# A spectral filter and MLP kernel: the first batch's last on-chip turn stores neighbouring channels side by side, and the transform stage behind it uses full 128-column tiles

## The chip, the core and the metric

The kernel runs on one core of a Trainium2 chip. Its engines work side by side, each through its own queue of instructions: TensorE (matrix products; PE in the profile, with its weight loads as PEld), VectorE (DVE), ScalarE (ACT), GpSimd (POOL) and the queue that issues DMAs (SP). The metric is the device time of one launch in microseconds. Three runs of the kernel gave a median of 740.99 us, the lowest 740.27 and the highest 742.85.

## The reference

Input `x` has 8 batches of 3008 rows by 256 channels. Along the rows each batch goes through a real Fourier transform, a product with a complex filter, and the inverse transform; then each row goes through a two-layer MLP with 256, 2048 and 256 channels.

```python
X = np.fft.rfft(x, axis=1)
Y = X * (filt_r + 1j * filt_i)[None, :, :]
y = np.fft.irfft(Y, n=x.shape[1], axis=1)
h = y.reshape(24064, 256) @ w_in
out = np.maximum(0.01 * h, h) @ w_out
```

## The kernel before

**The transform.** 3008 is written as 94 times 32. A transform is two stages of small matrix products with a turn (a change of which index lies on the partitions) between them: `s1` (94 points), turn, `s2` (32 points), filter product, `sa` (inverse, 32 points), turn, `sb` (inverse, 94 points). The output of `sb` lands in `yt`, which holds channels on the partitions and rows along the free axis, as the MLP needs them.

**Two forms of it.** Batches 1 to 7 make their turns by DMA and run inside the MLP's work. Batch 0 has nothing to run beside: it is a prologue written out by hand as the list `FIRST` (lines 482 to 500), in which each entry is a step and its arguments, and every engine's queue has its instructions in the order of that list. Its turns are DVE transposes of 32x32 blocks: `t1` (line 396) between `s1` and `s2`, and `t2` (line 442) between `sa` and `sb`, four instructions each, of 128 partitions by 1024 fp32 words. A word is a pair of fp16 values, so that one transpose moves two values at a time.

**The steps that the change touches.** `sae` (line 438, engine ACT in all 12 entries of `FIRST`) copies a result of `sa` from PSUM to `big[2]` as fp16 pairs. `t2 i` turns a quarter of the channels from `big[2]` to `big[0]`: `t2 0` and `t2 1` make the first half of the channels (`dt` 0), `t2 2` and `t2 3` the second. `sb_matmuls` (line 447) reads `big[0]` as the stationary operand of the last stage, with the constant `i1_sb` streaming by (94 columns); it is called by `sbp` (line 456) in the prologue and by `late_sb` (line 464) afterwards. `sbe` and `quad_copy` (lines 461 and 345) copy a group from PSUM to `yt` on ACT or DVE. One group is four values of the index n2 for one half of the channels; batch 0 has 16, of which ten (eight with `dt` 0, two with `dt` 1) are in `FIRST` and six (`dt` 1) are put among the work of the MLP's first chunks by the list `REST` (lines 114 and 703).

**The order at the end of the prologue.** On DVE: the last filter products (`s2d`), `t2 1`, `t2 0`, `t2 3`, `t2 2`, then the copies `sbe 0 3` and `sbe 1 0`. On PE: the last `sa` products, four matmuls without use (`warm 4`, which only keep PE at work), the eight groups with `dt` 0, `sbp 1 0` and `sbp 1 1`, then the MLP. On ACT: the `sae` copies, then eight `sbe` copies with `sbe 1 1` last.

**After the prologue.** The MLP runs over 47 chunks of 512 rows (`moe1`, line 520, is its first layer). A planner gives each piece of work a time (8 units to a chunk) and issues the pieces in the order of these times, with `work` as a heap; the times set nothing but the order in each queue. The first matmul of `moe1` needs the groups 0 and 1 of `dt` 0 in `yt`, its second those of `dt` 1.

Of the kernel before, what the change touches and what calls it, by code (L numbers as in the profile page):

```python
# [13 lines left out]
FP32 = mybir.dt.float32  # L14
# [5 lines left out]
N1, N2 = 94, 32  # L20
NC = 24
Q = 32
# [56 lines left out]
def kernel(  # L79
# [9 lines left out]
    nc = tc.nc  # L89
# [46 lines left out]
    i1_sb = cpool.tile([P, N2, NW], FP16, name="i1_sb")  # L136
# [8 lines left out]
    big = [cpool.tile([P, Q * D + (HALF // 2 if i == 2 else 0)], FP16, name=f"big{i}") for i in range(3)]  # L145
# [144 lines left out]
    def paired(t):  # L290
        return t[:].rearrange("p (e n t) -> p n e t", n=Q, t=2)
# [5 lines left out]
    E4 = D // 2 // 4  # L297
# [77 lines left out]
    held, spare = {}, [scrp.tile([P, 4, DH], FP32, tag=f"p{i // 2 + 1}", name=f"spare{i}") for i in range(6)]  # L375
# [61 lines left out]

    def sae(hf, c, e):
        engine[e](paired(big[2])[:, ds(c, 4), ts(hf, DH // 2)],
                  held.pop(("sa", hf, c)).rearrange("p n (t e) -> p n e t", t=2))  # L440

    def t2(i):
        a = big[2][:].bitcast(FP32)[:, ts(i, E4 * Q)].rearrange("p (e n r) -> p e n r", n=Q // 2, r=2)
        o = big[0][:].bitcast(FP32).rearrange("p (h n e r) -> p h e n r", h=2, n=Q // 2, r=2)
        nc.vector.transpose(o[:, i // 2, ts(i % 2, E4)], a)

    def sb_matmuls(ps, dt, h):
        assert ("i1t",) not in issued
        src = big[0][:].rearrange("p (h n e r t) -> p h n r t e", h=2, n=Q // 2, r=2, t=2)
        for j in range(4):  # L450
            n2 = 4 * h + j
            for t in range(2):
                nc.tensor.matmul(ps[64 * t : 64 * t + 64, j, :], src[:, dt, n2 // 2, n2 % 2, t, :],
                                 i1_sb[:, n2, :N1], start=True, stop=True)

    def sbp(dt, h, b):
        ps = fill(("sb", dt, h), b, 4, NW)[:, :, :N1]
        held["sb", dt, h] = ps
        sb_matmuls(ps, dt, h)
# [4 lines left out]
    def late_sb(dt, h, copy):  # L464
        ps = bank("pf", 4, NW)[:, :, :N1]
        sb_matmuls(ps, dt, h)
        quad_copy(0, h, dt, ps, copy)
# [11 lines left out]
    def blank(i):  # L479
# [19 lines left out]
        sbe 0 3 D, sbe 1 0 D  # L499
    """  # L500
    steps = dict(s1p=s1p, s1e=s1e, t1=t1, s2p=s2p, s2d=s2d, s2a=s2a, s2m=s2m, sap=sap, sae=sae, t2=t2,
                 sbp=sbp, sbe=sbe, x=load_x, w_out=load_w_out, xc=round_x, warm=keep_warm, blank=blank)
    for step in FIRST.split(","):
# [227 lines left out]
    for b in range(1, B):  # L731
        z = 47 * (b - 4) if b > 4 else 0
        p = PLANS[min(b, 4) - 1]
# [23 lines left out]
    while queue:  # L757
        time, n, stage, b, g, f = heapq.heappop(queue)
        t = max(time, last + GAP)
# [64 lines left out]
```

## Time and profile before

| | |
|---|---|
| median of 3 runs | 740.99 us (740.27 to 742.85) |
| the profiled execution | 740.64 us |
| its span, first to last instruction | 738.8 us |
| PE busy | 730.5 us (99%) |
| ACT busy | 549.3 us (74%) |
| DVE busy | 508.7 us (69%) |
| granted TensorE clock, mean over the span | 1.000 |
| prologue, up to the first MLP matmul | 34.71 us |

The 1.8 us between span and time lie outside the instructions. A line of a group names the source line, the engine, the operation, what it writes and reads with the shapes, how often, then the busy time and the mean duration of one in ns, and the idle time ahead of it. The chain of waits follows the execution back from its last instruction; what lies on it sets the end.

### The profile page before, as it was taken

The numbers are of one execution on the slowest core, as the hardware profiler recorded it, in microseconds if no ns is written. First come the engines' busy times: TensorE is split into PE (matmuls) and PEld (weight loads), VectorE is DVE, ScalarE is ACT, GpSimd is POOL, SyncE is SP. The second block draws the span as 40 slices with busy tenths as digits, with TensorE's granted clock in tenths as the row PEclk, the third lists the DMA queues.
The fourth block names the chain that finished last, engine by engine and source line by source line (L and its number), as shares of the span: only waits on it lengthen the run. The fifth ranks groups of instructions, "written<-read, shape, count | busy, mean of one in ns | idle before, by whom it ended". The sixth has DMA issues, their size and how long they took to land.

```text
span 738.8 us, 19530 instructions
## 1 busy us (share of the span) xinstructions
PE 730.5 (99%) x8129; PEld 521.8 (71%) x8129; DVE 508.7 (69%) x696; ACT 549.3 (74%) x763; POOL 168.0 (23%) x171
## 2 busy tenths in 40 slices
PE   8999999999999999999999999999999999999997
PEld 3666677777777777777777777777767777777776
DVE  7878557776677667676777668666767676465566
ACT  4775787887788778887688777888767777777762
POOL 5605411333221312212132322222031220000000
PEclk9999999999999999999999999999999999999999
DMA  9978778778755595556855477434863433112012
GB/s 203 228 109 171 189 150 170 178 172 167 188 134 126 138 193 143 130 145 126 183 131 137 122 157 169 115 90 110 149 172 95 117 106 94 55 55 66 29 46 71
DMA packets 128617, 98.44 MB, mean 133 GB/s; under 512 B 59296, under 2 KB 107296, under 8 KB 128336
## 3 DMA queue, kind: packets, MB, share of 16 engines
q1 hardware_dynamic: 112905, 79.37, 42.0%
q0 software_dynamic: 15056, 17.50, 15.7%
q8 instruction: 63, 1.03, 0.6%
q10 hardware_dynamic: 567, 0.32, 0.2%
q14 instruction: 26, 0.21, 0.1%
HBM read 45.97 MB, written 35.65 MB: 110 GB/s over the span
## 4 chain that ended last, share of the span: by engine, by line
PE 93%; SPq 2%; DMA 2%; DVE 1%; ACT 1%; POOL 0%; issue 0%; POOLq 0%
PE ph L528 42%; PE pf L601 18%; PE po_ps L601 18%; PE pf L269 2%; PE pf L362 2%; PE pf L315 2%; PE pf L337 2%; PE pf L693 1%; DMA x_sb<-in_x_dram 1%; PE po_ps L693 1%; SPq L277 1%; SPq L587 1%; DMA p_b_g<-p_b_g 1%; PE po_ps L384 0%; PE pf L436 0%; ACT yt L351 0%
## 5 line engine op out<-in xcount | busy, mean ns | idle before, releaser
L531 ACT ACTIVATE gt_c<-ph 128x1024 f16<-128x1024 f32 x376 | 385.4, 1025 | 132.3 <-PE ph L528 125.5
L528 PE MATMUL ph<-yt,w_in_sb 128*128 128x512 f16 x1504 | 447.3, 379 | 0.2 <-ACT yt L351 0.2
L601 PEld LDWEIGHTS <-gt_c 128*128 128x128 f16 x2800 | 201.8, 98 | 97.9 <-issue 1.3
L330 POOL TENSOR_TENSOR y_b_g<-p_b_g,p_b_g 128x512 f16<-128x512 f32 x84 | 118.1, 1407 | 421.1 <-DMA p_b_g<-p_b_g 288.1
L601 PEld LDWEIGHTS <-big 128*128 128x128 f16 x2128 | 151.4, 98 | 65.9
L528 PEld LDWEIGHTS <-w_in_sb 128*128 128x128 f16 x1504 | 117.7, 98 | 4.4 <-DVE yt L351 0.4
L324 DVE TENSOR_TENSOR p_b_g<-pf,fb_sb 128x512 f32<-128x512 f32 x78 | 53.7, 688 | 33.8 <-PE pf L315 20.3
L601 PE MATMUL po_ps<-wt_sb,gt_c 128*128 128x128 f16 x704 | 71.8, 219 | 0.0
L601 PE MATMUL pf<-wt_sb,gt_c 128*128 128x128 f16 x688 | 69.3, 219 | 0.0
L601 PE MATMUL pf<-wt_sb,big 128*128 128x128 f16 x704 | 68.7, 219 | 0.0
L601 PE MATMUL pf<-w_out_sb,gt_c 128*128 128x128 f16 x720 | 68.1, 219 | 0.0
L351 ACT CAST yt<-pf 128x376 f16<-128x376 f32 (+9 forms) x136 | 58.1, 441 | 12.2 <-PE pf L362 8.5
L601 PE MATMUL po_ps<-w_out_sb,gt_c 128*128 128x128 f16 x688 | 65.7, 219 | 0.0
L601 PE MATMUL po_ps<-wt_sb,big 128*128 128x128 f16 x688 | 65.5, 219 | 0.0
L567 DVE TENSOR_TENSOR gt_c<-gt_c 128x2048 f16<-128x2048 f16 x43 | 56.9, 1322 | 1.0
L327 DVE TENSOR_TENSOR p_b_g<-pf,fa_sb 128x512 f32<-128x512 f32 x84 | 57.2, 681 | 0.2
L567 DVE TENSOR_TENSOR big<-gt_c,big 128x2048 f16<-128x2048 f16 (+1 forms) x45 | 56.4, 1254 | 0.0
L567 DVE TENSOR_TENSOR big<-big,gt_c 128x2048 f16<-128x2048 f16 (+1 forms) x45 | 56.3, 1252 | 0.1
L567 DVE TENSOR_TENSOR big<-gt_c 128x2048 f16<-128x2048 f16 (+1 forms) x46 | 56.3, 1224 | 0.0
L339 ACT CAST big<-pf 128x512 f16<-128x512 f32 x84 | 49.0, 584 | 9.3 <-PE pf L337 7.4
L270 ACT CAST big<-pf 128x384 f16<-128x384 f32 x90 | 43.0, 479 | 11.5 <-PE pf L269 8.2
L362 PE MATMUL pf<-i_sb,big 128*128 128x94 f16 x448 | 37.0, 206 | 0.0
(98 smaller groups left out, 644.7 us busy)
## 6 DMA issues: line engine op xcount, KB each, us to landing
p_b_g<-p_b_g SPq DMA_DIRECT2D x156, 128.0 KB
out_dram<-ost_c_h SPq DMA_DIRECT2D x118, 128.0 KB
dz<-big SPq DMA_DIRECT2D x42, 256.0 KB
big<-dz SPq DMA_DIRECT2D x56, 192.0 KB
x_sb<-in_x_dram POOLq DMA_DIRECT2D x40, 192.0 KB, 4.2
x_sb<-in_x_dram POOLq DMA_DIRECT2D x2, 768.0 KB, 9.2
w_in_sb<-in_moe_w_in_dram POOLq DMA_DIRECT2D x1, 1024.0 KB, 13.1
w_out_sb<-in_moe_w_out_dram POOLq DMA_DIRECT2D x1, 1024.0 KB, 14.3
```

Source lines behind the costliest of these rows:

```text
L269: nc.tensor.matmul(ps[:, j, :], x_sb[:, 4 * h + j, ts(dt, P)], fwd1m[:, :NW], start=True, stop=True)
L270: copy(turn_in[:, :, dt, :, ds(4 * h, 4)], ps.rearrange("p n (q k) -> p k q n", q=4))
L324: nc.vector.tensor_tensor(p2[:], ps, fb, AL.mult)
L327: nc.vector.tensor_tensor(p1[:], ps, fa, AL.mult)
L330: ("y", b, g), lambda: nc.gpsimd.tensor_tensor(y1[:], p1[:], p3[:], AL.add)))
L339: nc.scalar.copy(st2[h % 3][:, ds(2 * (g % 2), 2), :], ps)
L351: copy(yt[:, dt, ds(to, 4 * n)].rearrange("p (a c) -> p a c", c=4), v[:, ds(a, n)])
L362: nc.tensor.matmul(ps[:, j, :], z2[h % 3][:, j, ts(dt, P)], i1_sb[:, 4 * h + j, :N1], start=True, stop=True)
L528: nc.tensor.matmul(ph[:, j, :], w_in_sb[:, dt, ts(ct, P)], yt[:, dt, ds(ci * CH % RING, CH)], start=(dt == 0), stop=(dt == NDT - 1))
L531: nc.scalar.activation(gts[ci][:, ds(2 * g, 2), :], ph, AF.Lrelu)
L567: nc.vector.tensor_tensor(*(v[:, ds(c0, n)] for v in (o, i0, i1)), op)
L601: nc.tensor.matmul(of[t], a()[:, c, ts(t, P)], w[:, c, :], start=(c == 0), stop=(c == NCH - 1))
```

## The change

Three places of the prologue's second half are rewritten. `sae` pairs the channels 2e and 2e+1 of its half of the channels, where it paired e and e+64; what it writes is the same set of addresses, what it reads from PSUM comes in order. `t2` writes its words in the order half, n2, e; before, two neighbouring values of n2 (r) lay side by side, in the order half, n2/2, e, r. So before, a DVE transpose stored 8 bytes (two words) at one place and then went 512 bytes on; now it stores 4 bytes (one word) and goes 256 bytes on. In `big[0]` the 128 channels of a half are now next to each other for each n2, so that `sb_matmuls` takes them as one stationary operand of 128x128 with the output on all 128 partitions of PSUM, where it took two of 128x64 (every fourth value), one for each 64 partitions. A group is four matmuls with four weight loads, where it was eight with eight. The number and order of the steps in `FIRST` and `REST` stay.

```diff
     def sae(hf, c, e):
         engine[e](paired(big[2])[:, ds(c, 4), ts(hf, DH // 2)],
-                  held.pop(("sa", hf, c)).rearrange("p n (t e) -> p n e t", t=2))
+                  held.pop(("sa", hf, c)).rearrange("p n (e t) -> p n e t", t=2))
 
     def t2(i):
-        a = big[2][:].bitcast(FP32)[:, ts(i, E4 * Q)].rearrange("p (e n r) -> p e n r", n=Q // 2, r=2)
-        o = big[0][:].bitcast(FP32).rearrange("p (h n e r) -> p h e n r", h=2, n=Q // 2, r=2)
+        a = big[2][:].bitcast(FP32)[:, ts(i, E4 * Q)].rearrange("p (e n) -> p e n", n=Q)
+        o = big[0][:].bitcast(FP32).rearrange("p (h n e) -> p h e n", h=2, n=Q)
         nc.vector.transpose(o[:, i // 2, ts(i % 2, E4)], a)
 
     def sb_matmuls(ps, dt, h):
         assert ("i1t",) not in issued
-        src = big[0][:].rearrange("p (h n e r t) -> p h n r t e", h=2, n=Q // 2, r=2, t=2)
+        src = big[0][:].rearrange("p (h n d) -> p h n d", h=2, n=Q)
         for j in range(4):
-            n2 = 4 * h + j
-            for t in range(2):
-                nc.tensor.matmul(ps[64 * t : 64 * t + 64, j, :], src[:, dt, n2 // 2, n2 % 2, t, :],
-                                 i1_sb[:, n2, :N1], start=True, stop=True)
+            nc.tensor.matmul(ps[:, j, :], src[:, dt, 4 * h + j], i1_sb[:, 4 * h + j, :N1], start=True, stop=True)
```

## The prediction

> **What bounds the kernel now.** I read the page first: which engine is full, and who carries the chain that ended last.
>
> ```profile
> PE 730.5 (99%) x8129; PEld 521.8 (71%) x8129; DVE 508.7 (69%) x696; ACT 549.3 (74%) x763; POOL 168.0 (23%) x171
> ...
> PE 93%; SPq 2%; DMA 2%; DVE 1%; ACT 1%; POOL 0%; issue 0%; POOLq 0%
> ```
>
> PE has 8.3 us without work in 738.8. Whatever lengthens or shortens PE's queue, or delays its start, therefore comes through to the end. The change touches only the prologue and six groups after it, so the next view is the chain of waits around the prologue's end (start, length, what):
>
> ```profile
> 27.90 1.22 DVE prod L416
> 29.11 2.29 DVE big L445 x2
> 31.45 0.46 PE pf L453 x8
> 31.93 2.74 ACT yt L351 x7
> 34.71 0.38 PE ph L528
> 35.09 0.38 PE ph L528
> ```
>
> The chain is not on PE here. It goes through two of the four transposes of `t2` (L445), one group of the last stage (L453), seven copies on ACT (L351), and then the MLP starts. The other two transposes run beside the ACT copies; the timeline of DVE shows how close behind they are:
>
> ```profile
> 30.19 3.55 DVE L445 STREAM_TRANSPOSE big<-big 128x1024 f32<-128x1024 f32 x3
> 33.66 0.51 DVE L351 CAST yt<-pf 128x376 f16<-128x376 f32 x1
> 34.35 0.55 DVE L351 CAST yt<-ph 128x376 f16<-128x376 f32 x1 [0.17 <-ACT yt L351]
> ```
>
> The fourth transpose ends at 33.74 (30.19 + 3.55), 1.35 us before the MLP's second matmul (35.09), which needs the last DVE copy. So all four transposes are within about a microsecond of the chain.
>
> **The transposes.** This term decides the sign. Their price, from the groups of the first 60 us:
>
> ```profile
> L416 DVE TENSOR_TENSOR prod<-ph,fa_sb 128x1024 f16<-128x1024 f32 x6 | 7.1, 1220 | 0.8 <-PE ph L408 0.6
> L445 DVE STREAM_TRANSPOSE big<-big 128x1024 f32<-128x1024 f32 x4 | 4.7, 1222 | 0.0
> L295 DVE CAST big<-pf 128x512 f16<-128x512 f32 x4 | 2.7, 688 | 0.5 <-PE pf L390 0.5
> L416 DVE TENSOR_TENSOR prod<-pf,fa_sb 128x512 f16<-128x512 f32 x4 | 2.5, 673 | 0.0
> L295 DVE CAST big<-ph 128x1024 f16<-128x1024 f32 x2 | 2.5, 1225 | 0.6 <-PE ph L390 0.6
> L351 DVE CAST yt<-pf 128x376 f16<-128x376 f32 x2 | 1.1, 531 | 0.0
> ```
>
> L416 with 512 and 1024 elements gives (1220 - 673) / 512 = 1.07 ns an element and 0.13 us fixed. L445 lies on the same line: 1024 words in 1222 ns. It stores two words at a place, so it opens a new place in SBUF every 2.14 ns. L295 also stores 4 bytes (two fp16 values) and then jumps, a place every 2.1 ns at full pace. None of the DVE rows that I read here opens places in SBUF faster than that. After the change each word is a place of its own.
>
> Lower end: the pace stays, nothing is added. L351 speaks for it: it reads PSUM with a jump at every element and still takes 376 x 1.07 + 0.13 = 0.53 us. A gain is left out, since L445 already runs at the pace of the in-order rows with fp32 on one side. Upper end: places open no faster than every 2.14 ns; 1024 of them take 2.19 + 0.13 = 2.32 us, 1.09 us more for each, 4.37 us for four. I take the upper end: L445 itself and L295 are stores into SBUF, as the changed instruction is, while L351's jumps are reads from PSUM. For two of the four I would have cover if only the first pair were on the chain; but DVE runs all four one after the other, and with 1.09 us more for each the fourth ends at 33.74 + 4.37 = 38.11. The groups with `dt` 0 and their seven ACT copies (2.74 us in the chain) begin 2.18 later than now, the copies at 34.1, so they are done by 36.9 and lie beside the second pair. The whole 4.37 is on the path.
>
> The Trainium skill bears on this term (Advanced Engine Details and Errata, section Memory Cachelines): SBUF has lines of 16 bytes, at least two accesses to a line are needed to hide its latency, and a new line for every access costs extra. It speaks against the change, with no figure; by it the four transposes cost something above nothing, and by the row alone the sum could also be the lower end's. No run shown so far has such a store.
>
> **Behind the fourth transpose.** Queued behind it on DVE are `sbe 0 3` and `sbe 1 0`; PE waits for it with `sbp 1 0` and `sbp 1 1`; SP and POOL have nothing waiting there. The stretch from its end to the MLP's second matmul stays, less what the shorter group saves, 0.10 us (from one execution of eight at 0.43 us to four at the 0.33 us of L269's form).
>
> **The late groups.** A piece of PE's queue with one group, before, and the same stage of a later batch, which already has four matmuls of 128x128:
>
> ```profile
> L453 PEld LDWEIGHTS <-big x128: 134/156/161, 31.4 to 80.1; 128*64 128x64 f16 x128
> ...
> 71.92 0.37 PE pf L453 x8
> ```
>
> ```profile
> L362 PEld LDWEIGHTS <-big x448: 97/98/99, 107.3 to 705.1; 128*128 128x128 f16 x150
> ...
> 107.54 0.17 PE pf L362 x4
> ```
>
> So each late group gives PE 0.37 - 0.17 = 0.20 us back. Six of them: 1.2 us. Two (at 41.4 and 45.8) stand ahead of or inside a stretch where the chain leaves PE for ACT and DVE (42.59 to 46.35), and I count them at nothing; that leaves 4 x 0.20 = 0.80. If the short wait for ACT at 69.3 also eats the two ahead of it, 0.40 is left. The other eight groups in the prologue lie beside the second pair of transposes: nothing.
>
> **The copies `sae`.** They read PSUM in order where they read with a jump. L295 on ACT has that read and the same store, 0.66 to 0.67 us for 128x512 against L439's 0.62 to 0.64. Bounds: 12 x 0.04 = 0.5 us more ACT work or none. It lies beside DVE's filter products and the first pair of transposes (ACT's last one ends at 31.34, the third transpose would start at 33.6). Without that cover it would be 0.04 us for the last copy. I count nothing.
>
> **Sum.** 4.37 - 0.10 - 0.80 = +3.47 us on the profiled execution's 740.64 (span 738.8, and 1.8 around it): 744.1 us. That execution is 0.35 below the median of 740.99, so the median may come out at 744.4. About 0.3%, 2.2 us, is what a measurement of this kernel can tell from no change.
>
> **Rivals.**
>
> *The transposes keep their pace.* A store that jumps at each word costs what L351's reads do. Then the chain goes as now, 0.10 us shorter at the first group, and the late groups give 0.80: 739.7 us, not slower. It decides from an added 0.9 / 4 = 0.23 us a transpose downwards. Against it: no row of SBUF stores with single words. Chance 0.18.
>
> *Part of the price.* Opening a place costs more, but half as much as the bound (0.55 us each, 2.2 in all), or part of the delay is absorbed behind the prologue: 2.2 - 0.9 = +1.3, 741.9 us. Against the absorbing: ACT's and DVE's queues start the MLP's work from the same point as PE, so the stretch from 42.59 to 46.35 moves with them, and the x loads and weights land early enough now. Chance 0.10.
>
> *The clock falls while PE waits.* With slow transposes PE has nothing from 31.24 (end of the four warming matmuls) to about 33.6, then 3 us of sparse groups, then about a microsecond of nothing. At the start of the trace, after idling, PE's weight loads of the warming matmuls come every 0.43 us (at 1.60, 2.02, 2.45 and so on to 5.44) and afterwards seven in 1.41 us: half rate for about 4.2 us. If that happened again at the MLP's start, 4.2 us would do 2.1 us of work: 744.1 + 2.1 = 746.2 us. Against it: no gap of the prologue now is over 0.4 us once PE has begun, so the trace does not show what one of 2.4 us does. Chance 0.10. The Trainium skill (TensorE: Matmul & The Clock Gate, Part 1) has the rate drop after a whole idle window of about 3.4 us; this gap would be shorter, which speaks against this rival.
>
> **How the numbers follow.** The forecast has 0.62; its own range is 743.0 to 745.0, from what the late groups give (0 to 1.2) and 0.1 us a transpose either way. The range for the time leaves out the rival in which the transposes keep their pace and the lower part of the partial price: 741.2 to 746.3 holds 0.62 + 0.10 + 0.08 = 0.80. Slower by over 0.3% (above 743.2 on the profiled time): 0.55 of the forecast, all of the clock's 0.10, 0.01 of the partial price: 0.66. Faster by over 0.3% needs more than the rival's 0.9 us: 0.03. Within 0.3%: 0.31.
>
> **What would show it.** L445 at about 2.3 us each, the fourth ending near 38.1, the MLP's second matmul at about 39.4 where it was 35.09; L453 with 64 instructions of 128x128 and weight loads of 98 ns; late groups of 0.17 us on the chain. The forecast is wrong if L445 stays at 1.2 us, if the MLP's second matmul moves by clearly less than the transposes grew, or if matmuls behind the gap are spaced at half rate.

## The result, and the profile after

Over 22 runs each the changed kernel has a median of 743.09 us and the kernel before 740.74: the ratio is 1.0032, with a 95% interval of 1.0025 to 1.0039, or about 2.35 us slower. The time lies inside the predicted range and on the predicted side; the forecast was 744.1 for the profiled execution, 1.2 us too high, and 744.4 for the median, 1.3 too high. Whether the loss is over the 0.3% bound the interval leaves open. The ratios in this document go by fast executions alone: one execution of a kernel below, `warm_gap2`, took 1544.55 us and is left out of its ratio.

The profiled execution took 742.86 us (span 741.0, so 2.2 more than before). First the two lines of the page that were shown of before: engines, and the chain by engine.

```profile
PE 729.8 (98%) x8065; PEld 521.1 (70%) x8065; DVE 513.3 (69%) x696; ACT 549.5 (74%) x763; POOL 167.0 (23%) x171
...
PE 91%; DMA 4%; DVE 2%; ACT 1%; POOL 1%; SPq 1%; issue 0%; POOLq 0%; DVEq 0%
```

PE has 64 matmuls fewer, and the chain gives DVE 2% where it gave 1%. Then the chain around the prologue's end (start, length, what; the last stage is now line 451, the MLP's matmul line 525, its activation line 528):

```profile
29.09 7.16 DVE big L445 x4
...
36.30 0.34 PE ph L451 x4
...
36.84 0.48 ACT yt L351
...
37.36 0.38 PE ph L525
...
38.43 0.32 PE pf L269 x4
38.75 0.85 PE ph L525 x2
```

All four transposes are on the chain, as forecast. They take 7.16 us where they took 4.63 (29.11 to 33.74): 2.5 us more, not 4.37. One of them takes 1.90 us in the median, before 1.22 (shortest, median and longest in ns):

```profile
L445 DVE STREAM_TRANSPOSE big<-big x4: 1874/1900/1972, 29.0 to 34.4; 128x1024 f32<-128x1024 f32 x4
```

The MLP's second matmul starts at 37.36, before at 35.09. Behind it is something that the sum did not have: from about 38 two matmuls of 512 columns take 0.85 us and four of 96 columns 0.32, where before they took 0.43 and 0.17. That is half rate. The windows show it as the granted clock. A row has the window and its length, then the busy time and the number of instructions of PE, PEld, DVE, ACT and POOL, and behind these five the clock:

```profile
34.00:38.00 4.00, 2.01 (x24) 1.22 (x24) 3.17 (x4) 2.35 (x6) 0.00 (x0) 1.00 1.11 190
38.00:42.00 4.00, 4.00 (x25) 2.20 (x24) 2.63 (x4) 2.21 (x3) 1.03 (x2) 0.57 1.44 200
```

and the second window in the kernel before:

```profile
38.00:42.00 4.00, 4.00 (x42) 2.25 (x40) 3.42 (x6) 4.00 (x7) 0.54 (x1) 1.00 1.42 202
```

The clock is 0.57 between 38 and 42 us, with 25 matmuls where before there were 42. PE was busy for only 2.01 of the 4 us ahead of it.

The late groups are the third part. One of them, on the chain of the changed kernel:

```profile
74.82 0.17 PE pf L451 x4
74.99 0.22 PE po_ps L690 x2
```

and the answering piece of the kernel before:

```profile
71.92 0.37 PE pf L453 x8
72.29 0.32 PE po_ps L693 x2
```

The group takes 0.20 us less, as forecast, and the piece behind it 0.10 less, which was not: after two tiles of 128x64 the next two matmuls took 0.32 us, after full tiles 0.22.

How these parts add up can be read from the starts of the MLP's activations, the same work in all kernels. A plus is the delay against the kernel before. The first activation stands at 36.16 before and at 38.53 after (+2.37), the fifth at 40.91 and 44.76 (+3.85), the 41st at 111.69 and 114.08 (+2.39). So the transposes, with the stretch behind them, cost 2.3 to 2.4 (2.27 at the MLP's second matmul), the half rate a further 1.5, and the late groups give 1.5 back. Later single waits for DMAs and for POOL move the two executions against each other by 0.2 to 1.3 us. They come at other places in other executions: in the kernel before, PE waits 1.2 us for POOL near 540 us, which the changed kernel does not.

### The profile page after: what moved, and what is told of

It is laid out like the page before. It is cut to its first block, busy times and chain, and to the rows that moved or that the text cites. A ratio compares the mean times of both kernels' runs of the same rounds, so it can differ in the third digit from the quotient of the medians.

```text
span 741.0 us, 19402 instructions
## 1 busy us (share of the span) xinstructions
PE 729.8 (98%) x8065; PEld 521.1 (70%) x8065; DVE 513.3 (69%) x696; ACT 549.5 (74%) x763; POOL 167.0 (23%) x171
## 4 chain that ended last, share of the span: by engine, by line
PE 91%; DMA 4%; DVE 2%; ACT 1%; POOL 1%; SPq 1%; issue 0%; POOLq 0%; DVEq 0%
PE ph L525 42%; PE pf L598 18%; PE po_ps L598 18%; PE pf L362 3%; PE pf L337 2%; PE pf L315 2%; PE pf L269 2%; DMA fa_sb<-in_filt_r_dram 1%; PE pf L690 1%; PE po_ps L690 1%; DMA fa_sb<-in_filt_i_dram 1%; DVE big L445 1%; ACT gt_c L528 1%; DVE prod L416 1%; DMA big<-dz 1%; SPq L277 1%
## 5 line engine op out<-in xcount | busy, mean ns | idle before, releaser
L528 ACT ACTIVATE gt_c<-ph 128x1024 f16<-128x1024 f32 x376 | 385.1, 1024 | 133.9 <-PE ph L525 127.0
L598 PE MATMUL pf<-wt_sb,gt_c 128*128 128x128 f16 x688 | 69.3, 219 | 0.0
L564 DVE TENSOR_TENSOR big<-gt_c 128x2048 f16<-128x2048 f16 (+1 forms) x46 | 58.3, 1268 | 0.0
```

The costliest lines, as they stand in the source:

```text
L528: nc.scalar.activation(gts[ci][:, ds(2 * g, 2), :], ph, AF.Lrelu)
L564: nc.vector.tensor_tensor(*(v[:, ds(c0, n)] for v in (o, i0, i1)), op)
L598: nc.tensor.matmul(of[t], a()[:, c, ts(t, P)], w[:, c, :], start=(c == 0), stop=(c == NCH - 1))
```

## The experiments

**The price of the store alone.** The kernel before with 16 more transposes in a stretch of DVE's queue.

```diff
+    def probe(i):
+        w = big[0][:].bitcast(FP32)
+        a = big[1][:].bitcast(FP32)[:, : E4 * Q]
+        # o: one of eight patterns of the same 1024 words in w
...
+        nc.vector.transpose(o, a)
-        s2p 0 12 4 1 b4, t1 2, s2d 0 8 4 1,
+        s2p 0 12 4 1 b4, t1 2, probe 0, probe 1, ..., probe 7, probe 7, ..., probe 0, s2d 0 8 4 1,
```

> The kernel before, with 16 more transposes on DVE ahead of the first s2d, each of 128x1024 words from big[1] into big[0], which t2 overwrites later; eight ways to store, each twice, in the order 0 to 7 and back. 0: two words at a place, places 512 bytes apart (before). 1: one word, 256 bytes apart (after). 2: one word, 512 bytes apart. 3: two words in one 16-byte line, 8 bytes apart from each other. 4: two neighbouring words, but every second pair across the border of two 16-byte lines. 5: words in order. 6: one word, 16 bytes apart. 7: four neighbouring words at a place. Theory 'line' (a store that opens a new 16-byte line with each word costs extra, two words in a line are enough): 0, 3, 5, 7 at 1.2 us, 1, 2, 6 at 1.9, 4 between them at about 1.55. Rival 'neighbours' (8 bytes must lie together): 3 at 1.9 and 4 at 1.2, the others as above. Rival 'distance' (banks or the stride decide): 1 and 2 differ, and 6 is near 1.2.

Timeline of its DVE queue, patterns 0 to 4 and 6 in order (start, length); 5 and 7 took 1.25 us:

```profile
19.11 1.25 DVE L509 STREAM_TRANSPOSE big<-big 128x1024 f32<-128x1024 f32 x1
20.39 1.95 DVE L509 STREAM_TRANSPOSE big<-big 128x1024 f32<-128x1024 f32 x1
22.38 1.92 DVE L509 STREAM_TRANSPOSE big<-big 128x1024 f32<-128x1024 f32 x1
24.33 1.25 DVE L509 STREAM_TRANSPOSE big<-big 128x1024 f32<-128x1024 f32 x1
25.61 1.49 DVE L509 STREAM_TRANSPOSE big<-big 128x1024 f32<-128x1024 f32 x1
...
28.41 1.98 DVE L509 STREAM_TRANSPOSE big<-big 128x1024 f32<-128x1024 f32 x1
```

The second pass, in reverse order, repeats this within 0.05 us. Theory "line" holds at every point: one word at a place costs 1.90 to 1.98 us at distances of 256, 512 and 16 bytes; two words in one line of 16 bytes cost 1.25 whether they touch or not; pairs of which every second one crosses the border of a line cost 1.49. "Neighbours" would have made the fourth pattern slow, and "distance" pattern 6 fast. The Trainium skill (Advanced Engine Details and Errata, section Memory Cachelines) says as much: lines of 16 bytes, and two accesses to a line needed. The price here is 0.65 to 0.73 us for 1024 words. With the added work the one execution of this kernel took 766.82 us.

**PE kept at work in the gaps.** The changed kernel with more warming matmuls.

```diff
-        ... sae 1 0 A, warm 4, sbp 0 1 b1,
+        ... sae 1 0 A, warm 10, sbp 0 1 b1,
-        ... sbp 0 5 b3, sbp 1 0 b4,
+        ... sbp 0 5 b3, warm 5, sbp 1 0 b4,
```

> The changed kernel with ten warming matmuls instead of four ahead of the first group of the last stage, and five more ahead of sbp 1 0; both fall into PE's idle time. Theory 'the clock fell in the gap and cost 1.5 us': the MLP's first matmuls come every 0.22 us from the start, the first MLP activation stands at about 38.5 as in the changed kernel but the third is 1.5 us earlier, and the time is 1.5 us below the changed kernel's 743.1, at about 741.6, a ratio of 1.0012. Rival 'the half rate was that one execution's or has another cause': no gain, 1.0032.

Measured: 740.6 us, ratio 1.0007 (0.9998 to 1.0015). The window that had 0.57:

```profile
38.00:42.00 4.00, 4.00 (x39) 2.34 (x38) 3.67 (x6) 3.40 (x5) 1.32 (x2) 1.00 1.41 200
```

Full clock and 39 matmuls. The transposes are as slow as in the changed kernel (7.29 us for four), the first activation is at +2.32, the fifth still at +2.32, the 41st at +0.86. So the half rate, and not something else behind the transposes, is the 1.5 us. Its share shows in the times as well: 1.0032 against 1.0007, with intervals that do not touch.

**Which gap.** The same two fillings apart (`warm 10` alone, and `warm 5` ahead of `sbp 1 0` alone).

> The changed kernel with ten warming matmuls instead of four ahead of the first group of the last stage; the second idle stretch of 1.5 us ahead of sbp 1 0 stays. If the second stretch is what lets the clock fall, the half rate stays (first MLP matmuls 0.43 us apart, ratio 1.0032); if PE's work over both stretches together decides, the clock stays up and the ratio is that of both fillings, 1.0007.

> The changed kernel with five warming matmuls ahead of sbp 1 0 alone; the first idle stretch of 1.0 us ahead of the first group stays. If the second stretch is the cause: full rate, ratio 1.0007. If the first one starts it: half rate, 1.0032.

With the first filling alone the ratio is 1.0016 (1.0003 to 1.0030), with the second alone 1.0005 (0.9991 to 1.0019). The window of 38 to 42 us, first of the first, then of the second:

```profile
38.00:42.00 4.00, 4.00 (x27) 2.24 (x26) 2.16 (x4) 1.51 (x2) 0.58 (x2) 0.61 1.44 196
```

```profile
38.00:42.00 4.00, 3.65 (x38) 2.06 (x35) 3.08 (x6) 2.50 (x4) 1.09 (x2) 1.00 1.48 199
```

In these two traces the second gap is the one that matters: PE's idle time of about 1.5 us ahead of `sbp 1 0`, which the slow second pair of transposes makes. The first, of 1.0 us in the changed kernel and 1.64 in the second of these two, does not bring the half rate by itself. The two intervals overlap, so the ratios alone do not decide it.

Two measurements say more. The first is the mean granted clock of every execution. In the 81 executions of the kernel before that ran beside these kernels it is never under 0.999; the changed kernel's profiled execution, with its one stretch of half rate, has 0.998. Taken as the sign of half rate, a clock of 0.998 or less is found in 21 of the changed kernel's 22 executions, in none of the 12 of `after_warm`, in 6 of 10 with the first filling alone, and in 1 of 9 with the second alone. Those 6 took 742.5 to 743.9 us, the other 4 took 740.1 to 741.2. So the same kernel gets the half rate in some executions and not in others, and both fillings make it rarer. (Nine of the changed kernel's executions have 0.995 or 0.996, more than one such stretch explains; no trace of one was kept.)

The second is when the clock changes. In the changed kernel it rises at 3.98 us, falls at 38.12 and rises at 41.53: the last two are 3.41 us apart, the first two ten times that. In every trace here the changes lie on such steps of 3.41 us, counted from the first rise, which comes at 3.98 to 7.16 us and so differs between executions. The step ahead of the fall and the step of half rate, in the changed kernel:

```profile
34.70:38.12 3.42, 1.53 (x18) 0.89 (x17) 2.58 (x4) 1.65 (x5) 0.00 (x0) 1.00 1.15 187
38.12:41.53 3.41, 3.41 (x20) 1.87 (x18) 2.51 (x4) 1.74 (x2) 0.66 (x2) 0.50 1.46 199
```

After the first rise, each step of the twelve traces in which PE was busy for 1.62 us or less is followed by half rate, and none with 1.67 us or more is (1.51 in the first of these two kernels; 1.77 in the second, with its gap of 1.64 us). So in these traces PE's work within one step decides, and not one gap by itself; a gap counts by where it lies in the steps.

**A gap in the kernel before.** Its four warming matmuls are left out.

```diff
-        ... sae 1 0 A, warm 4, sbp 0 1 b1,
+        ... sae 1 0 A, sbp 0 1 b1,
```

> The kernel before without its four warming matmuls, which makes an idle stretch of some 1.3 us on PE ahead of the first group. Theory 'a stretch of one to one and a half us without PE work is enough for the half rate': MLP's first matmuls at 0.43 us for some 3 us, about 1.5 us more, ratio 1.0020. Rival 'it takes longer or sparser work than that': no half rate, ratio 1.0000.

Measured: ratio 1.0011 (1.0000 to 1.0022), and 1.00 as the granted clock from 38 to 42 us; the first, the fifth and the 41st activation stand at +0.73, +0.73 and +0.71. So no half rate in the profiled execution, and no execution of the ten has a mean clock under 0.999. This execution was late for another reason: POOL's last product and ACT's copies stood ahead of the third transpose on the chain. PE's idle pieces there were 0.49 and 0.56 us, shorter than I had expected, so that this kernel did not make the gap it was meant to make. Whether its 0.8 us are the missing matmuls' doing stays open.

**The new store with the old tiles.**

```diff
-                  held.pop(("sa", hf, c)).rearrange("p n (e t) -> p n e t", t=2))
+                  held.pop(("sa", hf, c)).rearrange("p n (t e) -> p n e t", t=2))
...
-        src = big[0][:].rearrange("p (h n d) -> p h n d", h=2, n=Q)
+        src = big[0][:].rearrange("p (h n e t) -> p h n t e", h=2, n=Q, t=2)
         for j in range(4):
-            nc.tensor.matmul(ps[:, j, :], src[:, dt, 4 * h + j], i1_sb[:, 4 * h + j, :N1], start=True, stop=True)
+            n2 = 4 * h + j
+            for t in range(2):
+                nc.tensor.matmul(ps[64 * t : 64 * t + 64, j, :], src[:, dt, n2, t, :],
+                                 i1_sb[:, n2, :N1], start=True, stop=True)
```

> The changed kernel's stores in t2 (one word at a place), but channels e and e+64 paired as before and the last stage in two tiles of 128x64 as before. Theory 'the transposes cost 2.4 us, the full tiles give back some 1.6 us in the late groups': late groups at 0.37 us and 0.1 us more for the piece of PE's queue behind them, as before; 1.6 us above the changed kernel if the clock falls here too, 744.7 or a ratio of 1.0054, and about 743.2 or 1.0033 if PE's longer groups keep the clock up. Rival 'the full tiles give only the 0.20 us of their own row': 0.8 us above the changed kernel with the same clock, 1.0043.

Measured: 743.69 us, ratio 1.0048 (1.0029 to 1.0067), too wide to choose between the cases by the time alone. The half rate is there (0.59 from 38 to 42 us). The first activation stands at +3.43, the fifth at +4.35. The first is higher than the changed kernel's because the transposes start 0.27 us later in this execution (29.36) and because the half rate begins at 37.83, so that a part of its cost lies ahead of the first activation. The 41st stands at +3.91. A late group of its chain, and the weight loads:

```profile
76.00 0.29 PE pf L453 x8
76.29 0.33 PE po_ps L693 x2
```

```profile
L453 PEld LDWEIGHTS <-big x128: 106/113/123, 33.1 to 84.0; 128*64 128x64 f16 x128
```

Here I had a detail wrong: I expected 0.37 us for a late group, and it is 0.29. With the new store the 64 channels of a tile lie every 4 bytes, before every 8, and a weight load of them takes 113 ns, not 156. So the late groups' 1.46 us (the fifth to the 41st activation) come in two parts: 0.44 from the closer channels, which this kernel already has, and the other 1.0 from the full tiles, about half of that in the piece behind the group, which keeps its 0.33. The Trainium skill (TensorEngine Tiling (Array Packing), section Key Properties) says that changing the tiling mode drains TensorE; the 0.10 us behind each group agree with that, but no run here shows that the drain is their cause.

**Half the change.** The channels with `dt` 1, whose last stage is mostly in the late groups, get the new store and full tiles; those with `dt` 0 stay as before.

```diff
     def t2(i):
+        if i < 2:     # dt 0: pairs of words, tiles of 128x64
+            a = a.rearrange("p (e n r) -> p e n r", n=Q // 2, r=2)
+            o = o.rearrange("p (n e r) -> p e n r", n=Q // 2, r=2)
+        else:         # dt 1: single words, tiles of 128x128
+            a = a.rearrange("p (e n) -> p e n", n=Q)
+            o = o.rearrange("p (n e) -> p e n", n=Q)
```

> Half the change: the channels with dt 1 (second pair of transposes, two groups in the prologue and the six late ones) as in the changed kernel, those with dt 0 as before. Theory: the second pair takes 1.2 us longer, its end comes at about 35.0 and the MLP's second matmul at about 36.2 (35.09 before); the late groups give 1.6 back and the clock stays up since the gap is short: 740.3, a ratio of 0.9995. Rival 'the clock falls also in a gap of half the length': up to 1.5 more, 1.0015.

> Half the change (dt 1 alone with single-word stores and full tiles), once more beside the next kernel: 0.9992 of the kernel before, 739.5 to 740.3.

Measured twice: 739.53 us with a ratio of 0.9992 (0.9983 to 1.0002), and 740.26 with 0.9992 (0.9982 to 1.0003). The transposes in the chain of the first:

```profile
29.04 6.06 DVE big L452 x4
```

Their end at 35.10 and the clock at 1.00 are as expected, but the reason that was given for the clock, a short gap, is wrong. PE's gap ahead of `sbp 1 0` is as long as in the changed kernel:

```profile
35.15 0.34 PE L460 MATMUL ph<-i_sb,big 128*128 128x94 f16 x4 [1.57 <-DVE big L452]
```

What differs is the work around it: in the two 3.41 us steps over the gap PE was busy for 2.31 and 2.39 us. In other executions the clock did fall. The mean clock is 0.998 or less in 5 of the 23 executions of both runs. The median of these 5 is 741.46 us, that of the other 18 is 739.43. So the rival is right for some executions.

The first and the fifth activation stand at +1.13, the 41st at -0.35. The delay is half of the changed kernel's, the gift of the late groups is whole. Beyond the 41st nothing of it should change, and 0.35 us of 740 (0.05%) is too little for these two runs to tell from nothing.

**PE's gap filled with work.** On top of the half, the `dt` 0 matmuls of the MLP's first four column tiles are issued in PE's gap.

```diff
+    def ahead(ct):
+        nc.tensor.matmul(wide[ct // 2][:, ts(ct % 2, CH)], w_in_sb[:, 0, ts(ct, P)], yt[:, 0, :CH],
+                         start=True, stop=False)
...
-        for dt in range(NDT):
+        for dt in range(1 if ci == 0 and ct < 4 else 0, NDT):
```

> Half the change as in the kernel hybrid, and PE's idle time ahead of sbp 1 0 filled with useful work: the first-half (dt 0) matmuls of the MLP's first four column tiles are issued there, and moe1 leaves them out; for that sbe 0 3 goes to ACT, and three groups take other PSUM banks. Theory: the second pair of transposes still ends at about 35.1, four matmuls of 0.215 us are off PE's queue behind it: 0.86 us below hybrid's 739.5 to 739.8, at about 738.8, a ratio of 0.9980. Rival 'ACT and DVE set the pace in the stretch behind the prologue and eat it': no gain over hybrid, 0.9992.

> Half the change, and the dt 0 matmuls of the MLP's first four column tiles issued in PE's idle time ahead of sbp 1 0 (moe1 leaves them out); in difference to hybrid_ahead sbe 0 3 stays on DVE, so that ACT has no ninth copy, and the group 0 5 goes to the bank of 0 7, 1 0 to that of 0 6, 1 1 to that of 0 5. Theory: the MLP's second-half matmuls begin at about 36.2 as in hybrid, and four matmuls of 0.215 us less stand behind them: 0.86 us below hybrid, a ratio of 0.998. Rival 'ACT and DVE set the pace in the stretch behind the prologue': first MLP activations 0.4 us earlier, but by the stretch around 44 us the lead over hybrid is gone, 0.9992.

In `hybrid_ahead` the copy of group 0 6 reads its PSUM bank after group 1 1 has overwritten it, so it computes wrong values there; the amount of work is the same. It took 740.26 us (0.9993; 0.9984 to 1.0002): moving `sbe 0 3` to ACT put a ninth copy on ACT, and PE waits for it. The timeline of its PE:

```profile
37.26 0.38 PE L544 MATMUL ph<-yt,w_in_sb 128*128 128x512 f16 x1 [1.31 <-ACT yt L351]
```

`hybrid_fill` leaves that copy on DVE: 740.04 us, ratio 0.9988 (0.9979 to 0.9996), the one kernel here whose interval lies wholly below 1. But it does not show the 0.86 us: its fifth activation is at +1.11, hybrid's at +1.13. Its chain says why:

```profile
37.40 0.89 ACT gt_c L547
...
38.31 1.02 ACT gt_c L547
39.33 0.37 ACT big L270
39.70 1.02 ACT gt_c L547
```

From 37.4 on ACT is the chain, one activation after the other, as the rival said. The other half of the rival, first activations 0.4 us earlier, did not come: the first stands at +1.24, hybrid's at +1.13. In this execution the third transpose waited for ACT copies that stood behind a late product of POOL, and the four end at 35.42, hybrid's at 35.10. Counted from the MLP's second-half matmuls (36.54 here, 36.21 in hybrid) the fifth activation comes after 5.47 us, in hybrid after 5.82: of the 0.86 us, 0.35 are kept up to there. Whether they last to the end stays open: against hybrid the difference of the ratios (0.0004) is within both intervals, and a part of it may be the clock, which is not under 0.999 in any execution of `hybrid_fill`.

## Why the prediction was right, and where it was not

The sign and the place are right: the new store makes the transposes slower, the four stand one behind the other on the path that starts the MLP, and all of their delay comes through. That the sum came near is partly luck: two errors cancel in part. The transposes' term was 1.9 us too large, and a half rate of 1.5 us that the sum did not have stood in its place. With the measured price alone the sum would have been 2.5 - 0.10 - 0.80 = +1.6 us. Of the signs of being wrong that the prediction names, one came: matmuls behind the gap at half rate. The wide range had room for such a mixture; the forecast's own range did not hold the profiled 742.86 us. That range was also mis-added: its two terms (0.4 us either way for the transposes, 0 to 1.2 for the late groups) give 743.3 to 745.3, not 743.0 to 745.0. And 743.2 is 0.3% above the median; above the profiled time it is 742.9.

*The transposes (4.37 forecast, 2.5 measured).* The step that failed is the upper end: "places open no faster than every 2.14 ns". That was the pace at which two words at a place happen to be stored, 2 x 1.07 ns, and not a limit on opening places. At one word a place the 1024 words take about 1.9 us, so a place opens every 1.73 ns ((1.90 - 0.13) / 1024). The rows bounded the price on both sides correctly, and the value lay between: the rival "part of the price" with 0.55 us each was nearer than the forecast (about 0.63 each here).

*Behind the fourth transpose (0.10 forecast, 0.24 measured).* From the end of the transposes to the MLP's second matmul it took 1.11 us (36.25 to 37.36), before 1.35. The mechanism held, and the size was off: before, the MLP's first matmul itself stood behind the ACT copies (34.71) and the second 0.38 behind it; now those copies are long done, the first matmul runs ahead, and only the last copies count.

*The clock (0 forecast, 1.5 measured).* I had this as a rival against the forecast, at 0.10 and with 2.1 us. It happened in the changed kernel's profile, together with the middle price of the transposes, and by the mean clock in 21 of its 22 executions; `after_warm` shows that work in the gaps removes it. The working had weighed the length of one gap of 2.4 us; with the faster transposes that gap was 1.0 us, and the second, of 1.54 us, which the working had put at "about a microsecond", left PE 1.53 us of work in the 3.41 us step ahead of the fall. The sentence on the Trainium skill (TensorE: Matmul & The Clock Gate, Part 1) pointed the wrong way here: by a whole idle window of about 3.4 us no drop was to come, and the measurement decides.

*The late groups (0.80 forecast, 1.46 measured).* The 0.20 us of the group's own row were right. Missing was the 0.10 in the next piece of PE's queue, and I counted four groups where five came through (between the fifth and the 41st activation the delay falls five times, by 0.29 to 0.32 us each, and rises once by 0.10): only the one inside the ACT- and DVE-bound stretch gave nothing, and the two ahead of 69.3 us gave theirs in full.

*`sae`.* Counted at nothing, and nothing it is: L439 takes 620 ns after, 618 before.

Put together, +2.37 at the first activation, +1.48 and -1.46, which is +2.39 at the 41st and close to the 2.35 of the medians.

## What to carry to other kernels

Look at what one instruction stores into each 16-byte line of SBUF: a DVE transpose of fp32 words that leaves a single word in each line runs some 50 to 60% longer, and two words in the line, touching or not, are enough to keep the pace. When a change delays a stage, ask what the engine that waits does meanwhile: a matmul engine with a gap ahead of its long stretch may start it at half rate, and here a few matmuls in the gap, useful or not, prevented it. Judge this by the clock of several executions: the same kernel had the half rate in some and not in others. When only part of the data gains from a layout, change only that part: here one half of the channels had the late groups' gain and the other half only the transposes' cost.

## What the runs showed of the hardware that was not expected

The clock changed in steps of 3.41 us, whose start differed between executions. In the changed kernel half rate came after a step with PE busy for 1.53 us, with no idle stretch over 1.54 us, and lasted one step (38.12 to 41.53); an idle stretch of 1.64 us in a step with 1.77 us of work (`warm_gap2`) did not bring it. A weight load of 128x64 took 156 ns with channels 8 bytes apart, 113 with 4 bytes, and a full 128x128 tile 99. Two matmuls that follow a group of 128x64 tiles took 0.10 us longer than after full tiles.
